# When the second batch's q/k units, the first batch's q tails and the second batch's v casts are prepared in a fused attention and MLP kernel

## The chip, the cores and the metric

The kernel runs on one core of a Trainium2 chip. Its time is device microseconds of one launch. The core has five engines that work side by side, each with its own in-order queue of instructions: TensorE (PE in the profile; PEld is its weight load), VectorE (DVE), ScalarE (ACT), GpSimd (POOL) and SyncE (SP), which issues most DMAs. An instruction waits on semaphores for what it needs, and everything behind it on its engine waits with it. SBUF is the on-chip memory; PSUM takes TensorE's results.

## The reference

Eight batches, eight heads, 576 positions, head dimension 64. Attention keeps, in each row, only the scores within tau of the row's largest; its output, laid out as 4608 tokens of 512 features, goes through a two-layer MLP.

```python
scores = scale * np.matmul(q, k.transpose(0, 1, 3, 2))
thresh = np.max(scores, axis=-1, keepdims=True) - tau
scores = np.where(scores >= thresh, scores, -1000000000.0)
scores = scores - np.max(scores, axis=-1, keepdims=True)
attn = np.exp(scores)
attn = attn / (np.sum(attn, axis=-1, keepdims=True) + 1e-09)
x = np.matmul(attn, v)            # then (batch, seq, heads * dim), flattened to tokens
h = x @ w_in                      # 512 -> 2048
g = np.maximum(0.01 * h, h)
out = g @ w_out                   # 2048 -> 512
```

## The kernel before, in words

**Steps.** A batch is 18 steps: two blocks of 256 rows, for each block four pairs of heads, for each pair two chunks of 128 rows (16 steps), and two steps for the last 64 rows of all heads ("tails"). Step n of the whole run counts from 0; the second batch is steps 18 to 35. The loop at the end of the kernel has one pass per step number, and the order in which it calls the helpers is the order of each engine's queue. The work of one step of attention is spread over several passes. "Step n" below means pass n of that loop where it speaks of a queue.

In pass n TensorE computes the scores of step n (L252); VectorE copies them out of PSUM with the minimum of the negated scores of each row, once per head ("the reduction", L260); the threshold is minimum plus tau (L269 on VectorE for steps 0 to 8 and 15 to 22, L272 on POOL otherwise). ScalarE does the exponentials of step n - 1 (L295, L291, L292) and VectorE the weights of the other head (L304, which reads two SBUF tiles). So the threshold of step n is needed by pass n + 1's L291 and L304.

**Weights to outputs.** For the first eight steps the weights are transposed on TensorE in pass n + 2 (`turn_w_pe`, L331, copied by L333), together with the reciprocals of their sums (L310), which L313 first widens to 64 columns: on VectorE in passes below 7, on POOL in passes 7 and 8. Later steps go in twos: reciprocal in the pass after the second one's weights, widening on POOL, one transposing DMA on SP's queue (L321). The product with v (pv, L348) and its scaling into x (L370) follow three passes after the second step of a two in the early steps, five passes otherwise.

**MLP.** When a block of 256 tokens has its x (pass 10 for the first, 20 for the second), layer 1 follows in eight units, one per pass (`layer1`, L391, with the activation L393 on ScalarE), and then layer 2, two units per pass (L407). In the passes 11 to 18 and 21 to 28 there is thus one layer 1 unit each.

**q and k.** They come as fp32 and are used as two fp16 parts, a high and a low one, transposed. A batch has ten units: k and q of the four pairs (k0, q0, k1, ... q3; 128x512 elements) and k and q of the tails (128x256). For the second batch POOL splits each unit in three pieces: `split_scale` (L137) and `split_high` (L143) in pass n_ - 3, `split_low` (L151) in pass n_ - 2; TensorE transposes it in pass n_ (`turn`, L186), and VectorE (the first seven units) or ScalarE copies it out of PSUM (L195, L189 for tails). The k tails are copied once more within SBUF, on POOL (L191). A `half` tile holds the two parts until they are transposed; four of them rotate. The last unit of the first batch, its q tails (`first[9]`), is split on POOL and transposed and copied in two passes of its own, given in the two `zip` lines. From the third batch on, units are transposed in another way (`turn_rows`).

**v.** `cast_v` (L106, two instructions per pair of heads) and `cast_vtails` (L111, two instructions) cast v to fp16 on POOL.

**Order within a pass on POOL.** The first entry of `pool_at[n]`, the threshold, the widening of the step pair that has ended, and then the other entries; the v casts are appended last. On TensorE: scores, the layer 1 unit, the turns, the early weights' transposes, layer 2, pv.

**PSUM tiles.** The tag "h" has two rotating tiles, shared by layer 1's outputs, by the turns of units and by half of the early weights' transposes. A new tile waits until the one before the last has been read.

```python
hp = ps.tile([128, nj, T], FP32, tag="h", bufs=2, name="hp")           # layer1
tp = ps.tile([128, 2, 2, 2, 64], FP16, tag=bank, bufs=2 if bank == "h" else 1, name="tp")   # turn, tails
```

Of the kernel before, what the change touches and what calls it, by code (L numbers as in the profile page):

```python
# [37 lines left out]
def kernel(  # L38
# [35 lines left out]
    def load_main(b, s, which, eng=None, parts=1):  # L74
        t = sb.tile([128, 4, 256], FP32, tag="raw", bufs=4, name="raw")
        n = 4 // parts
        for i in range(parts):
            (eng or nc.sync).dma_start(
                out=t[:, ds(n * i, n), :],
                in_=SRC[which][b, ds(4 * s + n * i, n), 0:MAIN, :].rearrange("h (p t) d -> p h (t d)", t=4))  # L80
        raws[b, s, which] = t

    def load_tails(b, which, engs=(nc.sync, nc.sync)):
        t = sb.tile([128, 2, 2, 64], FP32, tag="rawt", bufs=2, name="rawt")
        src = SRC[which][b, :, MAIN:S, :].rearrange("(u sh) p d -> u p sh d", u=2)
        for u in range(2):
            engs[u].dma_start(out=t[ds(64 * u, 64), :, :, :].rearrange("p s h d -> p (s h) d"), in_=src[u])
        tails[b, which] = t

    def load_v(b, s):  # L90
        t = sb.tile([128, 4, 256], FP32, tag="vraw", bufs=2, name="vraw")
        nc.sync.dma_start(out=t[:, :, :], in_=v[b, ds(4 * s, 4), 0:MAIN, :].rearrange("h (p t) d -> p h (t d)", t=4))
        vraws[b, s] = t

    def load_vtails(b):
        t = sb.tile([128, NP, 64], FP32, tag="vrawt", bufs=1, name="vrawt")
        src = v[b, :, MAIN:S, :].rearrange("(r h) p d -> h p r d", h=2)
        for h in range(2):
            nc.sync.dma_start(out=t[ds(64 * h, 64), :, :], in_=src[h])
        vtails[b] = t  # L100

    def cast_v(b, p):
        src = vraws[b, p // 2][:, ds(2 * (p % 2), 2), :].rearrange("p h (t d) -> p h t d", d=64)
        dst = v16[b % 2][:, p, :, :].rearrange("p (h t) d -> p h t d", h=2)
        for h in range(2):
            nc.gpsimd.tensor_copy(out=dst[:, h, ds(h, 4), :], in_=src[:, h, :, :])  # L106

    def cast_vtails(b):
        t = vtails.pop(b)
        for h in range(2):  # L110
            nc.gpsimd.tensor_copy(out=v16[b % 2][ds(64 * h, 64), :, 4 + h, :], in_=t[ds(64 * h, 64), :, :])  # L111
# [17 lines left out]
    def split_scale(key):  # L129
        t = sb.tile([128, 4, 2, 64], FP32, tag="scaled", bufs=2, name="scaled")  # L130
        if key[1] == "t":
            src = tails[key[0], key[2]][:, :, :, :]
            dst = t[:, 0:2, :, :]
        else:
            src = pair_of(*key)
            dst = t[:, :, :, :].rearrange("p t h d -> p h t d")
        nc.gpsimd.tensor_scalar(out=dst, in0=src, scalar1=64.0, scalar2=1.0, op0=AX.mult, op1=AX.mult)  # L137
        scaled[key] = t

    def split_high(key):  # L140
        n = 2 if key[1] == "t" else 4
        halves[key] = new_half()
        nc.gpsimd.tensor_copy(out=halves[key][:, 0, 0:n, :, :], in_=scaled[key][:, 0:n, :, :])  # L143

    def split_low(key):

        n = 2 if key[1] == "t" else 4
        m = 2 if key[0] < 2 else n
        src = scaled.pop(key)
        for i in range(0, n, m):  # L150
            nc.gpsimd.tensor_tensor(out=halves[key][:, 1, i : i + m, :, :], in0=src[:, i : i + m, :, :],  # L151
                                    in1=halves[key][:, 0, i : i + m, :, :], op=AX.subtract)
# [18 lines left out]
    def turn(key, copy=None, bank="h"):  # L171
        copy = copy or nc.scalar.copy
        b, p, which = key
        dst, half = turned_of(b, which), halves.pop(key)
        n = 2 if p == "t" else 4
        c0 = 0 if which == "q" else 64
        if p == "t":
            c0 = MAIN if which == "q" else 0
            tp = ps.tile([128, 2, 2, 2, 64], FP16, tag=bank, bufs=2 if bank == "h" else 1, name="tp")
        else:  # L180
            tp = ps.tile([128, 2, 4, 128], FP16, tag="h", bufs=2, name="tp")
        for x in range(2):
            for t in range(n):
                for h in range(2):
                    o = tp[ds(64 * h, 64), x, :, t, :] if p == "t" else tp[ds(64 * h, 64), x, t, :]
                    nc.tensor.transpose(o, half[:, x, t, h, :], ident[:, :])  # L186
        if p == "t":
            src = tp[:, :, :, :, :].rearrange("d x u s p -> d x (u s) p")
            copy(out=dst[:, :, :, ds(c0, 64)], in_=src)  # L189
            if which == "k" and b:  # L190
                nc.gpsimd.tensor_copy(out=dst[:, :, :, 576:640], in_=dst[:, :, :, 0:64])  # L191
            elif which == "k":
                nc.vector.tensor_copy(out=dst[:, :, :, 576:640], in_=src)
        else:
            copy(out=dst[:, :, p, ds(c0, 512)], in_=tp[:, :, :, :].rearrange("d x t p -> d x (t p)"))  # L195
# [233 lines left out]
    loads_at, turns_at, pool_at = {}, {}, {}  # L429

    def at(d, n, f):
        d.setdefault(n, []).append(f)

    def units(b):
        u = [(b, p, w_) for p in range(NP) for w_ in "kq"]
        return u[:2] + [(b, "t", "k")] + u[2:] + [(b, "t", "q")]
# [3 lines left out]
    for b in range(1, B):  # L440
        base = PERB * (b - 1)
        for i, (s, w_) in enumerate(((0, "k"), (0, "q"), (1, "k"), (1, "q"))):
            at(loads_at, base + ((-2, 0, 5, 7)[i] if b > 1 else (3, 4, 8, 9)[i]),
               lambda b=b, s=s, w_=w_: load_main(b, s, w_))
        for i, w_ in enumerate("kq"):
            at(loads_at, base + (1, 3)[i] if b > 1 else (6, 16)[i], lambda b=b, w_=w_: load_tails(b, w_))
        for i, key in enumerate(units(b) if b == 1 else ROWS):
            n_ = 9 + 3 * i // 2 if b == 1 else base + (5, 7, 9, 9, 11, 13, 15, 17, 19, 21)[i]
            key = (b,) + key[-2:]
            at(pool_at, n_ - 3, lambda key=key: split_scale(key))  # L450
            at(pool_at, n_ - 3, lambda key=key: split_high(key))
            at(pool_at, n_ - 2, lambda key=key: split_low(key))
            if b == 1:
                at(turns_at, n_, lambda key=key, i=i: turn(key, nc.vector.tensor_copy if i < 7 else None))
            else:
                at(rows_at, n_, key)
    for b in range(B):
        base = PERB * (b - 1)
        if b:
            for s in range(2):  # L460
                at(loads_at, base + 11 + 3 * s, lambda b=b, s=s: load_v(b, s))
            at(loads_at, base + 13, lambda b=b: load_vtails(b))
        for p in range(NP):
            at(pool_at, base + 15 + 2 * p if b else 2 + p, lambda b=b, p=p: cast_v(b, p))
        at(pool_at, base + 16 if b else 2, lambda b=b: cast_vtails(b))

# [35 lines left out]
    def split_pool(key):  # L504
        split_scale(key)
        split_high(key)
        split_low(key)
# [8 lines left out]
    first = units(0)  # L516
# [8 lines left out]
    for key in first[4:6]:  # L525
        split_high_act(key)
        split_scale(key)
        split_low(key)
    for n_, key in zip((1, 2, 6), first[7:]):
        at(pool_at, n_, lambda key=key: split_pool(key))  # L530
    for i in range(8):
        at(pool_at, i if i < 2 else 1 + i // 2 if i < 6 else i, lambda i=i: load_w(i))
    at(turns_at, 0, lambda: turn(first[3], nc.vector.tensor_copy))
    for n_, key in zip((1, 2, 3, 8), first[5:8] + first[9:]):
        at(turns_at, n_, lambda key=key: turn(key, nc.vector.tensor_copy if key[2] == "q" else None))

    N = len(steps)
# [103 lines left out]
```

## Time and profile before

| | |
|---|---|
| median of three runs | 495.36 us (494.4 to 495.49) |
| profiled execution, its own time | 495.17 us |
| its span, first to last instruction | 493.4 us |
| mean granted TensorE clock | 0.998 |
| busy: TensorE, VectorE, ScalarE, POOL | 96%, 83%, 88%, 65% of the span |
| busy from 30 to 45 us, of 15 | TensorE 11.64, VectorE 14.55, ScalarE 13.28, POOL 12.85 us |
| busy from 78 to 92 us, of 14 | TensorE 14.00, VectorE 12.26, ScalarE 13.32, POOL 9.79 us |

A row of the timeline gives start, length, engine, line, operation, output and inputs, how many, and in brackets how long the engine stood idle before and who ended that. A row of the chain gives start, length and what the end of the program hung on then. The scores of pass 9 begin at 39.85 us, of pass 12 at 48.09, of pass 15 at 57.82, of pass 21 at 75.39 and of pass 30 at 102.28; a pair of passes takes 6.2 us from about pass 38 on.

### The profile page before, as it was taken

To read this page: it belongs to the slowest core of one execution; us is meant where nothing else is said; L and a number is where in the kernel's file an instruction comes from. 1 tells how busy PE (TensorE), PEld (TensorE's weight loads), DVE (VectorE), ACT (ScalarE), POOL (GpSimd) and SP (SyncE) were. 2 spreads that over 40 slices of the span, in tenths; PEclk is the share of its full clock that TensorE was granted. 3 is DMA by queue.
4 is the path that set the end of the run, shared out by engine and by line. 5 is a ranking of instruction groups with operands and counts; after the bars stand their busy time and mean duration, and the time that the engine had idled before them with its cause. 6 is when DMAs were issued, how large, how long until landed. Compare 5 with 4: busy or idle time off the path is not lost.

```text
span 493.4 us, 19704 instructions
## 1 busy us (share of the span) xinstructions
PE 475.3 (96%) x8039; PEld 344.0 (70%) x8039; DVE 409.1 (83%) x1195; ACT 433.2 (88%) x784; POOL 319.4 (65%) x545
## 2 busy tenths in 40 slices
PE   8977899999999999999999999999999999999996
PEld 7655666757677777777777777767777777667884
DVE  4999999998989898999889898989989898788100
ACT  6898899999999999999999999999999999999431
POOL 5997898778766786768766777677767683222000
PEclk9999999999999999999999999999999999999999
DMA  8998698999998999999998999999999988769412
GB/s 251 261 203 144 132 191 178 217 178 189 219 197 158 204 210 199 174 182 232 161 210 162 216 194 191 196 170 228 164 206 163 195 150 163 130 117 163 108 45 66
DMA packets 220444, 87.79 MB, mean 178 GB/s; under 512 B 190656, under 2 KB 217280, under 8 KB 220352
## 3 DMA queue, kind: packets, MB, share of 16 engines
q1 hardware_dynamic: 217120, 82.00, 82.2%
q0 software_dynamic: 2688, 4.19, 4.9%
q8 instruction: 63, 1.03, 0.9%
q10 hardware_dynamic: 544, 0.33, 0.2%
q14 instruction: 29, 0.24, 0.2%
HBM read 36.70 MB, written 9.44 MB: 94 GB/s over the span
## 4 chain that ended last, share of the span: by engine, by line
PE 80%; DVE 7%; ACT 5%; DMA 4%; POOL 2%; issue 1%; SPq 0%; DVEq 0%; POOLq 0%
PE hp L391 26%; PE o L407 20%; PE sc L252 20%; PE pv L348 7%; PE osc L407 4%; DVE s L260 3%; DMA wT<-w 3%; PE tpr L207 3%; DVE w L304 2%; ACT w L292 1%; ACT e L295 1%; DMA raw<-in_k_dram 1%; ACT s L291 1%; POOL half L151 1%; DVE x L370 1%
## 5 line engine op out<-in xcount | busy, mean ns | idle before, releaser
L260 DVE TENSOR_SCALAR_CACHE_REDUCE s<-sc 128x576 f32<-128x576 f32 x288 | 206.4, 754 | 33.8 <-PE sc L252 31.6
L252 PE MATMUL sc<-kT,qT 64*128 64x288 f16 (+1 forms) x1920 | 135.0, 285 | 3.7 <-DVE s L260 2.6
L391 PE MATMUL hp<-x,win 128*64 128x256 f16 x2048 | 136.7, 275 | 1.3 <-DVE x L370 1.0
L391 PEld LDWEIGHTS <-win 128*64 128x64 f16 x2560 | 118.7, 109 | 24.2 <-issue 18.4
L272 POOL TENSOR_SCALAR th<-mn 128x2 f32<-128x2 f32 x127 | 57.6, 454 | 110.9 <-DVE s L260 79.9
L407 PE MATMUL o<-wout,g 128*64 128x512 f16 x992 | 127.8, 379 | 0.0
L304 DVE SCALAR_TENSOR_TENSOR w<-s,th,e 128x576 f16<-128x576 f32 x144 | 122.9, 854 | 0.5 <-ACT e L295 0.5
L252 PEld LDWEIGHTS <-qT 64*128 64x128 f16 (+1 forms) x1920 | 76.6, 96 | 57.8 <-issue 42.7
L292 ACT ACTIVATE w<-s,minus_tau 128x576 f16<-128x576 f32 x144 | 111.7, 775 | 4.9
L291 ACT ACTIVATE s<-s,th 128x576 f32<-128x576 f32 x144 | 110.3, 766 | 2.8 <-POOL th L272 2.5
L295 ACT ACTIVATE e<-s,mn 128x576 f16<-128x576 f32 x144 | 110.2, 765 | 0.3 <-DVE s L260 0.3
L393 ACT ACTIVATE g<-hp 128x512 f16<-128x512 f32 x144 | 84.0, 583 | 26.9 <-PE hp L391 26.6
L151 POOL TENSOR_TENSOR half<-scaled,half 128x512 f16<-128x512 f32 (+1 forms) x91 | 89.3, 988 | 2.0
L407 PEld LDWEIGHTS <-g 128*64 128x64 f16 x1152 | 65.2, 110 | 30.1 <-issue 0.5
L348 PE MATMUL pv<-wT,v 128*64 128x256 f16 (+1 forms) x960 | 52.1, 247 | 1.9 <-DMA wT<-w 1.9
L348 PEld LDWEIGHTS <-v 128*64 128x64 f16 x960 | 41.6, 111 | 15.4 <-issue 1.4
L137 POOL TENSOR_SCALAR scaled<-raw 128x512 f32<-128x512 f32 x62 | 44.3, 714 | 5.9 <-DMA raw<-in_k_dram 4.8
L143 POOL CAST half<-scaled 128x512 f16<-128x512 f32 (+1 forms) x74 | 43.4, 587 | 4.5
L313 POOL CAST w<-rec 128x256 f16<-128x256 f32 (+1 forms) x70 | 32.6, 466 | 6.7 <-DVE rec L310 5.0
L106 POOL CAST v<-vraw 128x256 f16<-128x256 f32 x64 | 31.8, 526 | 1.3
L370 DVE TENSOR_TENSOR x<-pv,wT 128x256 f16<-128x256 f32 x64 | 27.1, 423 | 4.5 <-PE pv L348 3.8
L292 ACT ACTIVATION_READ_ACCUMULATOR w<-s,minus_tau 128x1 f32 x144 | 26.9, 187 | 0.0
(55 smaller groups left out, 321.7 us busy)
## 6 DMA issues: line engine op xcount, KB each, us to landing
vraw<-in_v_dram SPq DMA_DIRECT2D x16, 512.0 KB, 5.2
out_dram<-osb SPq DMA_DIRECT2D x16, 512.0 KB, 3.4
raw<-in_k_dram SPq DMA_DIRECT2D x14, 512.0 KB, 4.8
raw<-in_q_dram SPq DMA_DIRECT2D x14, 512.0 KB, 4.7
win<-in_moe_w_in_dram POOLq DMA_DIRECT2D x4, 512.0 KB, 7.0
wout<-in_moe_w_out_dram POOLq DMA_DIRECT2D x4, 512.0 KB, 11.0
wT<-w SPq DMA_TRANSPOSE x68, 6.1
raw<-in_k_dram SPq DMA_DIRECT2D x4, 256.0 KB, 5.4
```

What stands on the lines that cost most here:

```text
L151: nc.gpsimd.tensor_tensor(out=halves[key][:, 1, i : i + m, :, :], in0=src[:, i : i + m, :, :], in1=halves[key][:, 0, i : i + m, :, :], op= ...
L252: nc.tensor.matmul(out=o, lhsT=lhs, rhs=turned[st.b, "k"][rows, kx, pair, ds(key0, 288)], start=(i == 0), stop=(i == 2), skip_group_check= ...
L260: nc.vector.tensor_scalar(out=st.s[:, h, :].rearrange("p (a b) -> p a b", a=2), in0=st.sc[h][:, :, 0:288], scalar1=-1.0 / UNIT, scalar2=No ...
L272: nc.gpsimd.tensor_scalar(out=st.th[:, :, 0], in0=st.mn[:, :, 0], scalar1=1.0, scalar2=tau_f, op0=AX.mult, op1=AX.add)
L291: nc.scalar.activation(out=z, in_=z, func=AF.Prelu, bias=st.th[:, h, 0:1], scale=-1.0, alpha=1e20)
L292: nc.scalar.activation(out=st.w[h], in_=z, func=AF.Exp, bias=minus_tau[:, :], scale=1.0, accum_out=st.sum[h])
L295: nc.scalar.activation(out=st.e[:, :], in_=st.s[:, h, :], func=AF.Exp, bias=st.mn[:, h, 0:1], scale=-1.0)
L304: nc.vector.scalar_tensor_tensor(out=st.w[0], in0=st.s[:, 0, :], scalar=st.th[:, 0, 0:1], in1=st.e[:, :], op0=AX.is_le, op1=AX.mult, accum ...
L348: nc.tensor.matmul(out=o, lhsT=v16[st.b % 2][:, 2 * c + u if st.tail else st.p, blk, :], rhs=rhs, start=(i == 0), stop=(i == 4), skip_grou ...
L391: nc.tensor.matmul(out=hp[ds(64 * u2, 64), jj, :], lhsT=w_in16[:, i, ds(128 * j + 64 * u2, 64)], rhs=g.x[:, i, :], start=(i == 0), stop=(i ...
L393: nc.scalar.activation(out=g.g[:, ds(nj * u, nj), :], in_=hp[:, :, :], func=AF.Prelu, bias=0.0, scale=1.0, alpha=0.01)
L407: nc.tensor.matmul(out=g.o[ds(64 * u2, 64), :], lhsT=g.g[:, j, ds(128 * m + 64 * u2, 64)], rhs=w_out16[:, j, :], start=(j == 0), stop=(j = ...
```

## The change

The same instructions are issued in another order.

- The second batch's ten units are turned in passes 11, 12, 13, 14, 16, 17, 19, 20, 21, 22 instead of 9, 10, 12, 13, 15, 16, 18, 19, 21, 22 (k0, q0, k tails, k1, q1, k2, q2, k3, q3, q tails), and split three and two passes ahead of that. The first two move by two passes, the next six by one, the last two stay.
- The first batch's q tails are split in pass 11 instead of 6, and turned in pass 13 instead of 8. In pass 13 the second batch's k tails are turned too, before them.
- The second batch's v is cast in passes 19, 21, 23, 25 (tails in 19) instead of 15, 17, 19, 21 (tails in 16).

```diff
         for i, key in enumerate(units(b) if b == 1 else ROWS):
-            n_ = 9 + 3 * i // 2 if b == 1 else base + (5, 7, 9, 9, 11, 13, 15, 17, 19, 21)[i]
+            n_ = base + (5, 7, 9, 9, 11, 13, 15, 17, 19, 21)[i]
+            if b == 1:
+                n_ = (11, 12, 13, 14, 16, 17, 19, 20, 21, 22)[i]
             key = (b,) + key[-2:]
...
         for p in range(NP):
-            at(pool_at, base + 15 + 2 * p if b else 2 + p, lambda b=b, p=p: cast_v(b, p))
-        at(pool_at, base + 16 if b else 2, lambda b=b: cast_vtails(b))
+            at(pool_at, 2 + p if b == 0 else base + (19 if b == 1 else 15) + 2 * p, lambda b=b, p=p: cast_v(b, p))
+        at(pool_at, 2 if b == 0 else base + (19 if b == 1 else 16), lambda b=b: cast_vtails(b))
...
-    for n_, key in zip((1, 2, 6), first[7:]):
+    for n_, key in zip((1, 2, 11), first[7:]):
         at(pool_at, n_, lambda key=key: split_pool(key))
...
-    for n_, key in zip((1, 2, 3, 8), first[5:8] + first[9:]):
+    for n_, key in zip((1, 2, 3, 13), first[5:8] + first[9:]):
         at(turns_at, n_, lambda key=key: turn(key, nc.vector.tensor_copy if key[2] == "q" else None))
```

## The prediction, made before the changed kernel was run

> **What bounds the kernel now.** I read the granted clock (0.998, nothing to explain there), the page's chain, the chain in order of time for the first 130 us, and the timelines of the five engines from 26 to 110 us. By the page the chain is TensorE's:
>
> ```profile
> PE 80%; DVE 7%; ACT 5%; DMA 4%; POOL 2%; issue 1%; SPq 0%; DVEq 0%; POOLq 0%
> ```
>
> All that the change touches lies before 100 us, and there TensorE is not yet the limit: it is busy 11.64 of the 15 us from 30 to 45, VectorE 14.55. From about step 38 every step has the same TensorE work (two steps take 6.2 us), so a microsecond won or lost earlier reaches the end whole. In order of time, the chain up to 78 us is VectorE's, with one transposing DMA in it; then TensorE's; then once more a DMA:
>
> ```profile
> 50.38 6.72 DMA wT<-w
> 57.11 0.04 issue
> 57.15 0.74 PE pv L348 x10
> ...
> 76.95 0.35 DVE x L370
> 77.30 0.04 issue
> 77.34 0.74 PE hp L391 x10
> ```
>
> 76.95 is the x of step 20, which releases layer 1. Whatever shift the change leaves there, TensorE carries on. What stands still before that, on ScalarE (first column: start; brackets: idle before, and who ended it):
>
> ```profile
> 41.93 1.29 ACT L333 COPY wT<-wp 128x640 f16<-128x640 f16 x2 [1.56 <-PE wp L331]
> ...
> 59.33 0.78 ACT L291 ACTIVATE s<-s,th 128x576 f32<-128x576 f32 x1 [0.94 <-POOL th L272]
> ```
>
> Both lead to POOL. Its queue:
>
> ```profile
> 38.77 0.30 POOL L313 CAST w<-rec 128x128 f16<-128x128 f32 x1
> 39.02 1.83 POOL L151 TENSOR_TENSOR half<-scaled,half 128x256 f16<-128x256 f32 x2
> ...
> 46.55 0.62 POOL L137 TENSOR_SCALAR scaled<-raw 128x512 f32<-128x512 f32 x1
> 47.24 0.61 POOL L143 CAST half<-scaled 128x512 f16<-128x512 f32 x1
> 47.93 1.30 POOL L151 TENSOR_TENSOR half<-scaled,half 128x256 f16<-128x256 f32 x2
> 49.32 0.58 POOL L272 TENSOR_SCALAR th<-mn 128x2 f32<-128x2 f32 x1
> ```
>
> One split of a q/k unit costs POOL 2.77 us (46.55 to 49.32). The widening of step 6's reciprocals at 38.77 waits behind splits, though the reciprocal ended at 37.12; TensorE waits 1.52 us for it. VectorE pays too: its weights operation (L304) takes 0.81 us beside a quiet POOL and twice that beside a splitting one:
>
> ```profile
> 35.30 1.54 DVE L304 SCALAR_TENSOR_TENSOR w<-s,th,e 128x576 f16<-128x576 f32 x1
> ...
> 38.57 1.75 DVE L304 SCALAR_TENSOR_TENSOR w<-s,th,e 128x576 f16<-128x576 f32 x1
> ...
> 42.92 0.81 DVE L304 SCALAR_TENSOR_TENSOR w<-s,th,e 128x576 f16<-128x576 f32 x1
> ```
>
> **The change, part by part.** No instruction is added or removed; only order changes, on POOL, VectorE, TensorE and, by one copy, ScalarE.
>
> *Steps 6 to 9, gain.* The splits of k0 and q0 and of the first batch's q tails leave POOL's steps 6 to 8; k0 starts in step 8. The weights of steps 5, 6 and 7 fall from 1.02, 1.55 and 1.76 to about 0.82, 0.82 and 0.95 (one split still beside the last), the tails' copy (0.32) leaves VectorE's step 8 and the two 0.6 us copies of k0 and q0 leave 9 and 10, and TensorE's 1.52 us wait goes. VectorE's reductions of steps 7, 8 and 9 then start at 33.55, 36.1 (held by scores, 0.95 after the previous reduction's end) and 39.5, against 33.75, 37.04 and 41.57; ScalarE's copies at 40.4 against 41.93. By step 11 the reduction starts near 44.6 instead of 47.28. The two DMAs for w_out behind the splits (0.82 us each) go out earlier. The transposing DMA of steps 8/9 goes out near 48.0 instead of 50.38, and TensorE's 1.23 us wait for it in step 14 is gone: late next there is the threshold.
>
> *Steps 9 to 12 on POOL, loss.* The work comes back here. From the end of step 9's reduction (40.9) POOL runs, in its new order: threshold 0.78 (0.15 after the reduction, 0.63), q0's split 2.77, threshold 0.26, k tails 1.65 (0.47 + 0.47 + 0.70), threshold 0.26, widening 0.40, scale and high of k1 1.38, the q tails 1.65, low of k1 1.38, threshold of step 12 0.26: 10.8 us, against three steps that VectorE would now do in 9. Beside it run three weights operations, and each costs the POOL instruction under it about 0.5 us (pairs of L151 at 1.82 and 1.69 against 1.30, at 53.43 and 57.33): 1.5. So step 12's threshold is ready at T = 40.9 + 10.8 + 1.5 = 53.2. ScalarE, free for it at 50.9, stands 2.3 us; before, it used it at 52.66 without waiting. Behind it wait ScalarE's activations, and VectorE's weights of step 12, with the copies behind those. Bounds for T: 50.9, where ScalarE needs it, and 54.2 (below).
>
> *Step 13, a new wait.* Step 13 takes three tiles of the PSUM tag h, which has two: layer 1, k tails, q tails. The q tails' transposes wait until ScalarE has read layer 1's tile, with step 14's scores behind them on TensorE. From T: activations 0.81, 0.77 and 0.57, transposes 0.3, scores 0.9: step 14's reduction starts at T + 3.4 = 56.6 (before 55.26). Then layer 1 1.0, k1's turn 0.6, pv 0.65 and scores 0.9 on TensorE (VectorE's 3.05 lies beside): step 15's reduction at T + 6.5 = 59.7, before 58.84: 0.85 us late. What was won has gone.
>
> *Steps 15 to 20: zero.* VectorE copies three turned units in these steps in both (before in 15, 16, 18; after in 16, 17, 19), 0.6 us each, and POOL has some 14.4 us of splits and casts there either way, so the weights' excess stays. k3's copy on ScalarE (0.9) moves from step 19 to 20, beside VectorE's 2.6 us step. Bounds: -0.4 to +0.6, one copy's worth.
>
> *The v casts.* In step 19 they lie ahead of splits that POOL does late, so the widening of step 21 may come 2 us later; its DMA (6.2 us median) lands near 88.8, and pv takes it at 88.41 plus the shift: zero, at worst 0.6. In step 25 one pair of casts (0.75) comes to lie before this:
>
> ```profile
> 95.99 1.16 POOL L151 TENSOR_TENSOR half<-scaled,half 128x512 f16<-128x512 f32 x1
> 97.24 0.19 POOL L272 TENSOR_SCALAR th<-mn 128x2 f32<-128x2 f32 x1
> 97.49 0.83 POOL L313 CAST w<-rec 128x256 f16<-128x256 f32 x1
> ```
>
> The reciprocal was ready at 96.97. POOL had 0.48 idle before step 26's threshold to take up part; the low part then meets the weights at 97.26. I take the widening to end at 98.7 instead of 98.32: 0.35 onto the DMA and the pv that TensorE waits for at 105.26. Bounds 0 and 1.2 (cast and one such meeting). No load moves on SP's queue, and the tiles that later loads overwrite are read a step or more ahead of them.
>
> Sum: 0.85 + 0 + 0.35 = 1.2 us on the profiled execution's 495.17 (span 493.4 and 1.77 around it), 496.4; the median of the runs stands 0.19 higher: 496.6.
>
> [...]
>
> **The rivals.** *POOL keeps up.* If the three weights operations cost POOL nothing and its short splits run a little closer, T falls to 50.9, where ScalarE no longer waits; step 15's reduction then starts at 57.4, 1.4 us early, and with the step 25 cast hidden the time is 494.0, faster. For it: at 45.85 and 51.61 the weights delayed only a threshold, by 0.4. Against it: from 60 to 80 us, with POOL busy throughout, each weights operation lengthened one POOL instruction by 0.4 to 0.58. It decides when T is under 51.0; the sign turns at T = 52.0.
>
> *Gain and loss cancel.* T near 52.2 (one hit) and the cast hidden: 495.4. This is also the case that the change does nothing: VectorE works off the same list by x of step 20. For it: POOL, VectorE and ScalarE each have nearly the same work up to 78 us.
>
> *POOL blocks fully.* Each hit costs the whole 0.82 instead of 0.5, T = 54.2, and 497.6 results. For it: the lows at 39.02 took 0.53 longer while the weights took 0.94 longer, 1.47 together. Against it: the hits seen on POOL alone stay under 0.6.
>
> **How the numbers follow.** Forecast case 0.46, of which about a third lies within 0.2% (0.99 us, about what a measurement of this kernel can tell from no change); POOL keeps up 0.24; cancelling 0.16; full block 0.14. Slower 0.30 + 0.14 = 0.44, same 0.16 + 0.16 = 0.32, faster 0.24. The forecast's own range is 495.6 to 497.7 (T by 0.5 each way, the casts 0 to 0.6). For 8 in 10 it goes from 493.8, most of the first rival, to 498.2, the full block with the worse casts.
>
> **What would show it.** Right: no ScalarE wait on the transposed weights at 40 us; step 11's reduction 2 to 3 us earlier; ScalarE waiting 1.5 us or more for POOL's threshold of step 12; TensorE's tail transposes waiting for ScalarE's g in step 13; x of step 20 later than 77.3. Wrong: POOL idle before step 12's threshold, the tail transposes passing at once, or x of step 20 before 76.3; or, with that x late, a pv of step 30 that has caught up.

## The result, and the profile after

The changed kernel takes 496.46 us (median of 12 runs, 495.8 to 497.8); the kernel before, in 12 runs beside it, 494.76. The ratio is 1.0036 (95% interval 1.0026 to 1.0046): slower by 0.36%, 1.3 to 2.3 us. The profiled execution has a span of 494.1 us.

The profile shows one execution. All twelve report their granted clock: seven between 0.994 and 0.997, at 495.8 to 496.5 us (the profiled one is among them, at 0.997), and five at 0.991 or 0.992, at 496.6 to 497.8 us. A stretch of 3.41 us at half clock, as the profile shows one below, takes 0.0035 off this figure (half of 3.41 us in a span of 494.1). The five thus lost more clock than the profiled execution; where, no trace here shows.

The two profiles began differently in the first 25 us, where both kernels issue the same work, so below, times are counted from the start of step 5's reduction (26.12 us in the trace before, 25.25 us after) where the two are compared. Start of the reduction, in us from there (the changed kernel and the one with idle matmuls below, which issue the same work up to pass 13, stand 0.27 us apart at step 9 by this count, so such differences are good to some 0.3 us):

| step | before | after | after minus before | forecast |
|---|---|---|---|---|
| 9 | 15.45 | 13.13 | -2.32 | -2.1 |
| 11 | 21.17 | 18.35 | -2.82 | -2.7 |
| 13 | 26.33 | 24.24 | -2.09 | |
| 14 | 29.14 | 31.03 | +1.89 | +1.3 |
| 15 | 32.72 | 34.73 | +2.01 | +0.85 |
| 21 | 51.10 | 52.37 | +1.27 | +0.85 |
| 31 | 80.83 | 82.28 | +1.45 | +1.2 |
| end | 467.27 | 468.88 | +1.61 | +1.2 |

The gain comes as forecast and is lost between steps 13 and 14. Before, POOL stood idle ahead of step 12's threshold:

```profile
51.61 0.63 POOL L272 TENSOR_SCALAR th<-mn 128x2 f32<-128x2 f32 x1 [0.67 <-ACT w L292]
```

POOL's timeline of the changed kernel, from step 9's threshold to step 12's, in part (first column start, then length):

```profile
39.97 0.62 POOL L272 TENSOR_SCALAR th<-mn 128x2 f32<-128x2 f32 x1 [0.61 <-DVE s L260]
40.67 0.62 POOL L137 TENSOR_SCALAR scaled<-raw 128x512 f32<-128x512 f32 x1
41.35 0.61 POOL L143 CAST half<-scaled 128x512 f16<-128x512 f32 x1
42.05 1.81 POOL L151 TENSOR_TENSOR half<-scaled,half 128x256 f16<-128x256 f32 x2
...
45.16 1.18 POOL L151 TENSOR_TENSOR half<-scaled,half 128x256 f16<-128x256 f32 x1
```

and from the same view later on:

```profile
48.30 0.91 POOL L137 TENSOR_SCALAR scaled<-rawt 128x256 f32<-128x256 f32 x1
...
49.76 1.92 POOL L151 TENSOR_TENSOR half<-scaled,half 128x256 f16<-128x256 f32 x3
51.76 0.19 POOL L272 TENSOR_SCALAR th<-mn 128x2 f32<-128x2 f32 x1
```

POOL goes from one instruction to the next between 39.97 and 51.95. Three rows are longer than their like: 1.81 instead of 1.30, 1.18 instead of 0.67, 0.91 instead of 0.40, each by 0.51, and each beside a weights operation of VectorE (at 42.13, 45.04 and 47.70). ScalarE's and TensorE's timelines show who waits (brackets):

```profile
51.99 0.78 ACT L291 ACTIVATE s<-s,th 128x576 f32<-128x576 f32 x1 [2.28 <-POOL th L272]
```

```profile
49.96 0.42 PE L186 MATMUL tp<-ident,half 128*64 128x128 f16 x8
54.20 0.41 PE L186 MATMUL tp<-ident,half 128*64 128x128 f16 x8 [3.81 <-ACT g L393]
54.54 1.62 PE L252 MATMUL sc<-kT,qT 64*128 64x288 f16 x12
56.09 1.92 PE L391 MATMUL hp<-x,win 128*64 128x256 f16 x16
57.80 0.68 PE L186 MATMUL tp<-ident,half 128*64 128x128 f16 x16
...
58.96 0.91 PE L252 MATMUL sc<-kT,qT 64*128 64x288 f16 x12
```

The first row is the k tails' turn, the second the q tails', 3.81 us later: the third h tile. What I had not foreseen are the two rows behind it: twelve score matmuls in 1.62 us (0.91 at 58.96) and a layer 1 unit in 1.92. Before, the same pieces of pass 14 took 1.05 and 1.06, and a wait of 1.23 us for the transposing DMA came behind them:

```profile
53.77 1.05 PE L252 MATMUL sc<-kT,qT 64*128 64x288 f16 x12
54.85 1.06 PE L391 MATMUL hp<-x,win 128*64 128x256 f16 x16
57.15 0.74 PE L348 MATMUL pv<-wT,v 128*64 128x256 f16 x10 [1.23 <-DMA wT<-w]
```

The table of the changed kernel by stretches (length, then the busy us of TensorE, its weight load, VectorE, ScalarE and POOL with their counts, then granted clock, DMA share, GB/s) has the reason:

```profile
50.00:54.00 4.00, 0.38 (x12) 0.24 (x7) 2.61 (x8) 1.98 (x4) 3.70 (x8) 1.00 0.58 113
54.00:58.00 4.00, 3.81 (x42) 2.65 (x43) 2.15 (x6) 2.34 (x5) 2.26 (x5) 0.57 0.94 105
58.00:62.00 4.00, 3.62 (x77) 2.69 (x74) 3.50 (x12) 3.89 (x7) 3.46 (x7) 1.00 0.73 194
```

The clock records say 0.5 from 54.51 to 57.92 us and 1.0 around it. The chain in order of time has, behind ScalarE's g, what answers to the 50.38 DMA of before:

```profile
54.20 0.41 PE tp L186 x8
54.61 1.55 PE sc L252 x12
56.16 1.85 PE hp L391 x16
```

The transposing DMA and the pv that waited for it have gone from the chain here; POOL's threshold, ScalarE's g, the tails' turn and two slow pieces of TensorE stand there instead.

### The profile page after: what moved, and what is told of

Same layout as the page of the kernel before. It is cut to its first block, busy times and chain, and to the rows that moved or that the text cites. A ratio compares the mean times of both kernels' runs of the same rounds, so it can differ in the third digit from the quotient of the medians.

```text
span 494.1 us, 19699 instructions
## 1 busy us (share of the span) xinstructions
PE 476.1 (96%) x8039; PEld 344.5 (70%) x8039; DVE 406.9 (82%) x1195; ACT 433.0 (88%) x784; POOL 317.5 (64%) x545
## 4 chain that ended last, share of the span: by engine, by line
PE 81%; DVE 8%; ACT 6%; POOL 2%; issue 1%; DMA 1%; DVEq 0%; POOLq 0%
PE hp L391 26%; PE sc L252 20%; PE o L407 20%; PE pv L348 7%; DVE s L260 4%; PE osc L407 3%; PE tpr L207 3%; DVE w L304 2%; ACT w L292 2%; DMA wT<-w 1%; ACT s L291 1%; ACT e L295 1%; POOL half L151 1%; PE tp L186 1%; PE idle L515 1%
## 5 line engine op out<-in xcount | busy, mean ns | idle before, releaser
L272 POOL TENSOR_SCALAR th<-mn 128x2 f32<-128x2 f32 x127 | 56.5, 445 | 108.0 <-DVE s L260 80.2
L304 DVE SCALAR_TENSOR_TENSOR w<-s,th,e 128x576 f16<-128x576 f32 x144 | 120.9, 840 | 1.5 <-POOL th L272 1.0
L313 POOL CAST w<-rec 128x256 f16<-128x256 f32 (+1 forms) x70 | 31.4, 449 | 12.5 <-DVE rec L310 11.7
```

The lines of the kernel that those rows point to most:

```text
L272: nc.gpsimd.tensor_scalar(out=st.th[:, :, 0], in0=st.mn[:, :, 0], scalar1=1.0, scalar2=tau_f, op0=AX.mult, op1=AX.add)
L304: nc.vector.scalar_tensor_tensor(out=st.w[0], in0=st.s[:, 0, :], scalar=st.th[:, 0, 0:1], in1=st.e[:, :], op0=AX.is_le, op1=AX.mult, accum ...
```

## The experiments

Ratios are to runs of the kernel before on the same chip, with 95% intervals. The runs were taken on several chips, on which the kernel before takes 494.76 to 495.14 us, so two kernels are compared by their ratios (the changed kernel: 1.0036). "In the trace" means from step 5's reduction, as above, in one profiled execution of each.

**The halved clock.** Filling matmuls in TensorE's wait:

```diff
+        if n_ == 13:
+            at(turns_at, n_, lambda: idle(40))
         at(turns_at, n_, lambda key=key: turn(key, nc.vector.tensor_copy if key[2] == "q" else None))
```

> The changed kernel, with 40 idle matmuls (128x128 on the identity, results unused) ahead of the q tails' turn in pass 13, where TensorE stood still for 3.8 us and its granted clock then was 0.5 for 3.4 us. If the halved clock costs time of its own: clock 1.0 throughout, step 14's scores 0.9 us instead of 1.62, its layer 1 unit 1.06 instead of 1.92, and step 15's reduction 6.6 us after step 12's threshold instead of 8.0; time about 495.2, 1.3 below the changed kernel's 496.46. Rival, the slow clock lies beside VectorE and ScalarE that set the pace anyway: clock 1.0, but the time stays at 496.4.

495.31 us, ratio 1.0000 (0.9992 to 1.0009). TensorE's timeline:

```profile
50.47 2.41 PE L515 MATMUL idle<-ident 128*128 128x128 f16 x40
54.36 0.41 PE L186 MATMUL tp<-ident,half 128*64 128x128 f16 x8 [1.49 <-ACT g L393]
54.70 0.91 PE L252 MATMUL sc<-kT,qT 64*128 64x288 f16 x12
55.54 1.06 PE L391 MATMUL hp<-x,win 128*64 128x256 f16 x16
```

The tails' turn waits until the same moment and ScalarE for its threshold as long (2.29 us), but the clock stays at 1.0 (from 50 to 58 us, in the changed kernel 0.57 from 54 to 58) and the scores take 0.91. Step 15's reduction starts 6.6 us after the threshold instead of 8.0. In the trace the end comes 1.25 us earlier than in the changed kernel (0.27 of it stands already at step 6), and the difference of the ratios is 0.36%. All eleven executions report a clock of 0.998 or more, those of the changed kernel 0.997 or less. So the clock alone carries about the whole difference to the kernel before; what is left of the change, early gain and later waits, sums to about nothing.

**The third tile, by place.** The q tails' turn two passes later:

```diff
-    for n_, key in zip((1, 2, 3, 13), first[5:8] + first[9:]):
+    for n_, key in zip((1, 2, 3, 15), first[5:8] + first[9:]):
```

> The changed kernel, with the first batch's q tails turned in pass 15 (which has no other turn) instead of 13; split in pass 11 as before. Theory (third h tile of pass 13 holds TensorE, then the clock): ScalarE still waits some 2.3 us for POOL's threshold of step 12, but TensorE's 3.8 us wait and the slow clock go; step 14's reduction about 2.5 us earlier; time about 494.6. Rival (the backlog on POOL alone makes the loss, TensorE's wait lies beside it): the gain is under 0.5 us, 496.0 or more. Rival (the later v casts or the units' later copies make the loss): 496.4.

496.02 us, 1.0011 (0.9999 to 1.0023). Step 14's reduction came 2.58 us earlier in the trace, as expected, and the rest did not:

```profile
51.34 0.89 PE L252 MATMUL sc<-kT,qT 64*128 64x288 f16 x11 [0.36 <-DVE s L260]
54.57 1.92 PE L391 MATMUL hp<-x,win 128*64 128x256 f16 x16 [2.35 <-ACT g L393]
...
61.99 0.93 PE L252 MATMUL sc<-kT,qT 64*64 64x288 f16 x24 [1.90 <-DVE qT L189]
```

The next h tile, layer 1's of pass 14, now waits for the same g; the clock falls at 54.10 all the same (its mean from 54.0 to 57.5 is 0.51). And the tails are needed by the scores of step 16, so with the turn in pass 15 these wait 1.90 us for VectorE's copy. The expectation missed both. The executions of this one kernel also price the clock without any edit: four of the twelve report 1.0 and take 494.3 to 495.0 us, near the time expected, and the eight at 0.992 to 0.997 take 495.8 to 497.4.

**The third tile, by tag.** The turn stays in pass 13 and takes a tile of the tag o:

```diff
-        at(turns_at, n_, lambda key=key: turn(key, nc.vector.tensor_copy if key[2] == "q" else None))
+        at(turns_at, n_, lambda key=key, n_=n_: turn(key, nc.vector.tensor_copy if key[2] == "q" else None,
+                                                     bank="o" if n_ == 13 else "h"))
```

> The changed kernel, with the q tails' turn of pass 13 in the PSUM tile of tag o, which is free in that pass, so that pass 13 takes two h tiles. Theory: the transposes no longer wait for ScalarE's g; step 14's scores and reduction come 2 to 2.5 us earlier; but ScalarE still waits 2.3 us for step 12's threshold, and layer 1's next tile (pass 14) then waits for the same g, so TensorE stands 2 us a little later and the clock may fall all the same. 494.8 to 495.5, 1.0 to 1.6 below the changed kernel. If the third h tile were the whole cause: 493.3 or less. If it mattered only through the clock and the clock falls again: 496 or more.

494.65 us, 0.9992 (0.9984 to 1.0001): 0.44% below the changed kernel, the time 0.15 us under the range expected. ScalarE still waits 2.30 us, TensorE 2.35 in pass 14, and the clock falls at 53.98 in the trace, where the layer 1 unit at 54.22 takes 1.92 us (seven of the eleven executions report 0.996 or less); but step 14's scores are through by then, and step 15's reduction comes 1.49 us earlier.

**POOL's backlog, by engine.** Step 12's threshold on VectorE:

```diff
-        if st.n < 9 or 15 <= st.n < 23:
+        if st.n < 9 or st.n == 12 or 15 <= st.n < 23:
```

> The changed kernel, with step 12's threshold alone computed on VectorE instead of POOL (0.2 us of VectorE more). Theory (the backlog on POOL ahead of this threshold holds ScalarE for 2.3 us, and through g of step 13 TensorE): ScalarE's wait falls under 0.5 us, TensorE's wait for g in pass 13 to about 1.5 us, too short to bring the clock down; time about 494.0. Rival (ScalarE's wait only moves to step 13's threshold, which is behind the same queue): gain under 1 us, 495.5 or more.

494.42 us, 0.9981 (0.9973 to 0.9990). ScalarE no longer waits for step 12, but 0.70 and 0.87 us for steps 13 and 14; TensorE's wait for g is 1.43 us, and the clock stays (0.999 in this execution):

```profile
51.87 0.41 PE L186 MATMUL tp<-ident,half 128*64 128x128 f16 x8 [1.43 <-ACT g L393]
52.22 0.91 PE L252 MATMUL sc<-kT,qT 64*128 64x288 f16 x12
```

0.55% below the changed kernel, the time 0.4 us above the one expected: part of ScalarE's wait does move on to later thresholds, as the rival had it. Against the kernel with idle matmuls, which keeps its clock too (1.0000), the shorter waits are worth about 0.2%, 0.9 us. In the trace it is 2.1 us at step 15, and more than half of that goes by the end, 0.8 us of it between steps 20 and 21, where pv waits 0.92 us for a transposing DMA.

**Both together**, tile and threshold.

> Both together: the q tails' turn in the tile of tag o, and step 12's threshold on VectorE. Theory (two causes, each of which holds ScalarE or TensorE in pass 13): neither wait is left, 493.0 to 493.8, close to the kernel with the q tails left in place (492.87). If a third cause is at work in the changed kernel: 494.4 or more, no better than the threshold alone (494.42).

493.96 us, 0.9975 (0.9967 to 0.9984). Neither wait of pass 13 is left (ScalarE still waits 0.72 and 0.82 us for the thresholds of steps 13 and 14), the clock stays (1.0 in this execution), and the reduction of step 15 starts at 30.10, against 30.32 with the q tails left in place (below). The time is 0.2 above the range expected: in the trace 0.8 us goes between steps 20 and 21, where pv waits 0.91 us for a transposing DMA, as above. The two causes account for what the changed kernel loses up to step 15; they do not add (0.44% and 0.55% alone, 0.61% together), and each of these gains holds some of the clock's.

**POOL's backlog, by order.** q tails split in pass 12, behind its threshold, and turned in pass 15:

```diff
-    for n_, key in zip((1, 2, 11), first[7:]):
+    for n_, key in zip((1, 2, 12), first[7:]):
...
-    for n_, key in zip((1, 2, 3, 13), first[5:8] + first[9:]):
+    for n_, key in zip((1, 2, 3, 15), first[5:8] + first[9:]):
```

> The changed kernel, with the first batch's q tails split in pass 12, behind its threshold, and turned in pass 15. Theory: step 12's threshold comes 1.65 us earlier than in the changed kernel, ScalarE waits about 0.6 us for it, TensorE's wait in pass 13 is gone; 493.0 to 493.8, below both kernels. Rival (POOL's total work up to pass 15 sets the pace wherever the pieces lie): ScalarE waits as long for step 13's or 14's threshold, 494.6 or more.

494.61 us, 0.9990 (0.9980 to 1.0001): 0.8 us above the range expected. Steps 14 and 15 start about where they do with the q tails left in place (26.64 and 30.15, there 26.81 and 30.32), though ScalarE waits 0.72, 0.36 and 0.83 us for the thresholds of steps 12 to 14, in part as the rival had it. Then the scores of step 16 wait for the tails' copy, and in the trace the clock falls once more:

```profile
59.07 1.65 PE L252 MATMUL sc<-kT,qT 64*64 64x288 f16 x24 [1.82 <-DVE qT L189]
60.65 1.90 PE L391 MATMUL hp<-x,win 128*64 128x256 f16 x16
```

That fall is not what made the time: ten of the twelve executions report 0.998 or more and take 493.8 to 495.2 us, the two at 0.996 take 494.6 and 495.2. What did is, as far as the trace shows, the wait for the copy: from step 15 to step 16 it is 5.07 us here, 2.66 with the q tails left in place. A turn in pass 14, a pass ahead of those that pay this wait, was not run.

**The parts alone.** Only the units moved (q tails and v casts as before):

> The second batch's units as in the changed kernel; the first batch's q tails (6 and 8) and the v casts as before. Theory: POOL's queue ahead of step 12's threshold is 1.65 us shorter, pass 13 has two h tiles, and the k0 and q0 splits have left passes 6 to 8, so most of the early gain stays: 493.3 to 494.3, below the kernel before. Rival (later units crowd VectorE's copies in passes 12 to 20): 495.5 or more.

492.87 us, 0.9962 (0.9948 to 0.9976), 0.4 below the range expected. Only the q tails moved (split 11, turn 13):

> Only the first batch's q tails moved (split in 11, turned in 13, where k1 is turned too); units and v casts as before. Theory: pass 13 has three h tiles, so TensorE waits there for ScalarE's g, 1 to 2 us, under what brings the clock down; POOL's 1.65 us of the tails now lie behind step 11's threshold and delay step 12's by about 1 us; against that the widening of step 6 comes 1 us earlier. 494.5 to 495.8. Rival (the third h tile alone makes the loss): 496 or more.

493.38 us, 0.9968 (0.9956 to 0.9979), 1.1 below the range expected. Only the v casts moved:

> Only the second batch's v casts moved; the rest as before. Theory: 494.8 to 495.1, no change or the 0.35 us of step 27's widening. Rival (the casts carry a part of the loss): 495.5 or more; rival (taking casts out of passes 15 to 17 relieves VectorE's weights there): 494.3 or less.

495.13 us, 1.0000 (0.9989 to 1.0011). And the changed kernel without them (all four have their edits from the change's diff):

> The changed kernel, with the v casts where the kernel before has them (15, 17, 19, 21, tails 16). Theory (the loss is made in passes 9 to 14): 496.1 to 496.5; at most 0.35 us lower, by the widening of step 27. Rival (the later casts hold POOL in passes 19 to 27): 495 or less.

497.16 us, 1.0031 (1.0019 to 1.0043); the time is 0.7 above the range expected, and four of its five executions report 0.991 or 0.992, but the ratio is that of the changed kernel. So the v casts do nothing that these runs can tell, and each of the other two moves alone makes the kernel faster by 0.3 to 0.4%. Step 9's reduction starts at 13.03 with the units alone, 13.35 with the q tails alone and 13.13 with both (before: 15.45): either one gives nearly the whole gain up to there. VectorE's weights in passes 6 to 8 agree: 1.01, 1.54 and 1.75 us before, 0.81, 0.81 and 0.85 with the units alone, 1.02, 1.01 and 1.08 with the q tails alone. By step 11 the q tails alone are 0.8 us behind the units alone (19.07 and 18.27). The costs, though, meet in passes 11 to 13. ScalarE's wait for step 12's threshold is

```profile
50.88 0.78 ACT L291 ACTIVATE s<-s,th 128x576 f32<-128x576 f32 x1 [0.71 <-POOL th L272]
```

for the units alone (2.28 us with both), and for the q tails alone, with step 13's in the second row,

```profile
50.54 0.78 ACT L291 ACTIVATE s<-s,th 128x576 f32<-128x576 f32 x1 [0.59 <-POOL th L272]
53.81 0.78 ACT L291 ACTIVATE s<-s,th 128x576 f32<-128x576 f32 x1 [0.45 <-POOL th L272]
```

with 1.13 us for step 14's behind them, TensorE's wait in pass 13 at 1.72 us, and no fall of the clock (0.998 in this execution, and 0.91 us for the scores behind the wait).

**Towards a better one.** Units moved, with the thresholds of steps 10 and 12 on VectorE:

```diff
-        if st.n < 9 or 15 <= st.n < 23:
+        if st.n < 9 or st.n in (10, 12) or 15 <= st.n < 23:
```

> Units as in the changed kernel, q tails and v casts as before, and the thresholds of steps 10 and 12 on VectorE; there ScalarE waited 0.62 and 0.71 us for POOL in the units' run. Theory: ScalarE sets the pace there, so most of 1.3 us is won: 491.8 to 492.4. Rival (VectorE is as full, and its 0.2 us a threshold and POOL's later thresholds eat it): 492.7 or more.

492.58 us, 0.9951 (0.9938 to 0.9963), 0.2 above the range expected and not told apart from the units alone: the waits come back at steps 13 and 14 (0.31 and 0.81 us). Units moved, q tails turned in pass 10 instead of 8:

> Units as in the changed kernel, v casts as before, q tails split in pass 6 as before but turned in pass 10, where no other unit is turned. Theory: the 0.32 us copy leaves VectorE's pass 8, but VectorE is held by the scores there or has it back in pass 10: 492.6 to 493.1, no difference to the units' run (492.87). Rival (VectorE's pass 8 sets the pace): 492.5 or less.

492.91 us, 0.9956 (0.9944 to 0.9969), no difference, as expected. The best kernels here are thus the unit move alone, with or without these edits: 0.4 to 0.5% below the kernel before.

## Why the prediction was right, and where it was not

The measured 496.46 us lie 0.14 under the forecast 496.6, but in part by luck. The forecast stood on 495.36 us for the kernel before, which took 494.76 beside the changed one; against that the change cost 1.7 us, not 1.2. And within the 1.2, errors cancelled.

- *The early gain*: right, -2.82 at step 11 against -2.7. The weights of steps 5, 6 and 7 took 0.81, 0.81 and 1.02 us (forecast 0.82, 0.82, 0.95), and ScalarE's wait for the transposed weights went.
- *POOL's queue of steps 9 to 12*: right. From the end of step 9's reduction (39.81) to step 12's threshold (51.95) it was 12.1 us, forecast 12.3, with three hits of 0.51 us on POOL where the rows of before gave 0.5. ScalarE waited 2.28 us, forecast 2.3. With the threshold on VectorE that wait went, 1.57 us of waits for the two next thresholds came, and 0.9 us were won with the clock kept in both: shown as a cause, and a smaller one than its length.
- *The rival "POOL blocks fully"* falls: its hit of 0.82, on which T = 54.2 stands, is in none of the three rows; each was longer by 0.51. In two of the three the collision shows on VectorE too, whose weights took 1.20 and 1.24 us at 42.13 and 47.70 instead of 0.81; at 45.04 they took 0.78. What decides which of the two pays, these rows do not show.
- *Step 13, the new wait*: right in kind, and the step that failed in size. It was written as "transposes 0.3, scores 0.9" and "layer 1 1.0" after the threshold; with the clock at 0.5 it was 0.4, 1.62 and 1.92, and step 15's reduction came 8.0 us after the threshold, not 6.5. The term left out is TensorE's clock, 1.0 to 1.4 us in the trace, by where one counts. I had read the clock as 0.998 before and said that there was nothing to explain, without asking what a wait of nearly four microseconds would do to it. The prediction named the wait that did this, of the tails' turn for ScalarE's g, and did not work out its length, 3.81 us.
- *Steps 15 to 20: zero*: off by 0.74 in the other direction; the shift fell from 2.01 to 1.27. In the trace before, VectorE also stood 0.6 us for scores in these steps, after it 0.4 for ScalarE, and its six weights summed to 6.1 us, after it 5.7. That lies outside the -0.4 to +0.6 of the prediction; how POOL's places brought it about was not tried.
- *The v casts*: 0.35 taken. The widening behind step 26's threshold came 0.36 us later than the shift of step 21, as forecast; of that 0.18 was left at step 31, since the DMA behind it took 6.59 us, not 6.78. In the traces with and without the casts' move they cost 0.2 to 0.4 us from step 21 to the end; the runs do not tell that from nothing.
- *"POOL keeps up"* and *"gain and loss cancel"*: the first did not happen. The second is what the kernel does once the clock is kept up (ratio 1.0000): in that trace the shift is +0.37 at step 15, -0.06 at step 21 and +0.36 at the end.

So the sum of the terms that I did write, 1.2, should have been near 0, and the term that I left out brought it to 1.7. The signs that I named came true, but for one that is open: x of step 20 began at 77.28 us in the trace's own time, not later than 77.3, and 1.27 us late counted from step 5. One statement of the prediction does not add up: T by 0.5 and the casts from 0 to 0.6 give 495.7 to 497.3 us, and the range was put at 495.6 to 497.7.

## What to carry to other kernels

Two moves that each win can lose together: either one had already emptied the crowded stage, and both put their work into the same next one. Before moving work on an in-order queue, sum what will stand ahead of each short instruction that another engine waits for (here a 0.2 us threshold behind 10 us of splits), and count the rotating tiles that one pass will take. Where the sum gives TensorE a wait of microseconds, price the slower clock behind it as well as the wait (here 3.81 us, and 3.41 us at half clock behind it).

## What the hardware showed that I had not expected

TensorE's clock fell behind stretches in which TensorE was partly busy. In the traces before and after, the records change at whole multiples of 3.41 us after the first rise (before: 7.21 us, then 491.90, which is 142 of them on; after: 6.72, then 54.51, which is 14 on, back at 57.92). Working out, from the matmul rows, TensorE's busy share in the emptiest such stretch before 130 us:

| kernel | emptiest full stretch | clock after it |
|---|---|---|
| changed | 0.09 | 0.5 |
| changed, v casts as before | 0.10 | 0.5 |
| q tails turned in 15 | 0.35 | 0.5 |
| q tails in tag o | 0.38 | 0.5 |
| split 12, turn 15 | 0.41 | 0.5 |
| v casts alone | 0.55 | 1.0 |
| before | 0.59 | 1.0 |
| q tails alone | 0.61 | 1.0 |
| threshold 12 on VectorE | 0.66 | 1.0 |
| idle matmuls | 0.69 | 1.0 |

In the other four kernels the emptiest stretch was busy 0.61 to 0.68, and the clock stayed. So a stretch that is busy up to 0.41 was followed by one at half clock, one that is busy 0.55 or more was not. At the end of the programs, where TensorE runs out of work, a stretch busy 0.13 was followed by half clock (before, from 491.90 us on), one of 0.48 (after, from 491.41 on) and one of 0.41 (idle matmuls) were not. The ends of matmuls are modelled, so the shares are not exact. The single waits do not tell it: I had counted on 1 to 2 us being too short, and 1.72 us (q tails alone) and 1.90 us (q tails turned in 15) did not bring the clock down, but 1.82 us did (split 12, turn 15). In these traces the fall thus goes with the busy share of one stretch of 3.41 us, which depends on where in it a wait falls, and not with the length of the wait alone. Executions of one kernel differ in their clock too: those with the q tails turned in pass 15 report 1.0 four times and 0.992 to 0.997 eight times, and seven of the 76 executions of the kernel before beside these experiments report 0.996 or less. Whether the place of a wait makes that difference as well is not shown; only one execution of each kernel was traced.
